# Transposing the query tile in two whole-tile instructions and a DRAM round trip, and a written-out order for all steps of the first MLP, in a linear-attention-then-two-MLPs kernel

## The chip, the cores and the metric

The kernel runs on one core of one Trainium2 chip. The metric is the device time of one execution in microseconds (us); smaller is better.

## The reference

Linear attention (8 batches, 8 heads, 576 positions, head size 64) is followed by two MLPs over the same 4608 tokens (512 to 2048 to 512 features).

```python
q_s = softmax(q, axis=-1)             # over the head's 64 features
k_s = softmax(k, axis=2)              # over the 576 positions
kv  = einsum('bhsd,bhse->bhde', k_s, v)
x   = einsum('bhsd,bhde->bhse', q_s, kv)      # -> (4608, 512)
x   = relu(x @ w_in1) ** 2 @ w_out1
h   = x @ w_in2
out = (h * sigmoid(1.702 * h)) @ w_out2
```

## The kernel before

**Precision and tiling.** Every large product is made in three passes of TensorE: an operand is cut into a rounded high part (`to_hi`, ScalarE) and the rest (`to_lo`, VectorE or GpSimd), and high*high, high*low and low*high are added up in PSUM. The first MLP goes over the tokens in 9 blocks of 512. In each block, 16 pieces `m{i}_{f}` (function `first`, tile `ph`, 12 matmuls of 512 columns) make hidden features, and 16 pieces `s{i}_{f}` (function `second`, tile `acc`, 12 matmuls) consume them `LAG = 2` pieces later. Between the two stand the steps `g.re`, `g.sq`, `g.hi`, `g.lo` (ReLU, square, and the two parts of the cut).

**What runs beside it.** While block i is multiplied, the attention of block i+1 is prepared, one pair of heads (p = 0 to 3) after another. The key steps `k{i}{p}.*` load k and v, find a maximum (`mx` on VectorE, `tr` on TensorE, `m2` on VectorE, `bc` on TensorE, `sb` on VectorE), take `ex` on ScalarE, multiply (`kv`, TensorE, tile `pk`), and normalise and cut the result (`su` on VectorE, `no` and `hi` on ScalarE, `lo` on GpSimd, tiles `kvn`, `kvh`, `kvl`). The query steps `x{i}{p}.*` load q, make its softmax (`mx`, `su` on VectorE, `sb`, `no` on GpSimd, `ex` on ScalarE), transpose it (`tr`), cut it (`hi` on ScalarE to `qh`, `lo` on VectorE to `ql`), multiply by the pair's `kvh` and `kvl` (`mm`, function `pe_x`, tile `px`) and put the result aside (`xe`). Near the end of a block `x{i}{p}.s` cuts the four results for the next block's `m` pieces. Besides this, the weights of the second MLP are widened from raw words (`w{n}.*`, tiles `ti`, `to`), stored, loaded again and turned into the seven combinations of a Strassen product (`f{n}.*`: sums `su` on VectorE, `hi` on ScalarE, `lo` on GpSimd, stores `d` by SyncE). The second MLP then uses these combinations.

**What sets the order.** Each engine works through its own queue in program order, and nearly all DMAs are issued by SyncE's queue (SP), which waits at a DMA until its data is there. The program of the opening (block 0, and the attention of block 1) follows a list written out by hand, `ORDER`. All steps after it are put into a list `plan` with planned times (for the attention the offsets `KV1` and `X1`, in units of `HS = 2.6` us, half of one m-and-s pair), moved by the amounts in `SHIFT`, and sorted by time.

**The transposition before.** For blocks 2 to 8 (7 blocks of 4 pairs: 28), `q_t` makes 16 VectorE transposes, each from one group of 32 partitions to another, so that features come to lie on partitions. The `qt` tile that they fill holds the tokens in another order than the products want, so `hi` and `lo` also put them in order: they write with a step of four elements (`by_token`). For blocks 0 and 1 TensorE transposes, and nothing of that changes.

Of the kernel before, what the change touches and what calls it, by code (L numbers as in the profile page):

```python
# [121 lines left out]
def kernel(  # L122
# [448 lines left out]
    def steps_x(i, p, ps, temp):  # L571

        st = {}
        G4 = P // 32
# [24 lines left out]
        def q_sum():
            r = st["m"][:, :, :, 1]  # L600
            nc.vector.reduce_sum(out=r, in_=st["q"], axis=AX.X)
            nc.vector.tensor_scalar_add(r, r, 1e-9)
            nc.vector.reciprocal(r, r)

        def q_norm():
            out = st["q"]
# [8 lines left out]
            st["qn"] = out

        def q_t():
            if i <= 1:  # L620
# [9 lines left out]
            st["qt"] = apool.tile([P, TB], F32, tag="qt", name=f"qt{i}_{p}", bufs=1)  # L630
            for a in range(G4):
                for g in range(G4):
                    h, e = divmod(g, 2)
                    nc.vector.transpose(  # L634
                        out=st["qt"][32 * g : 32 * g + 32, a * P : (a + 1) * P].rearrange(
                            "d (j t) -> d j t", j=QJ
                        ),
                        in_=st["qn"][32 * a : 32 * a + 32, h, :, 32 * e : 32 * e + 32],
                    )
            st["in"], st["out"] = "d (a j t) -> d a j t", "d (a t j) -> d a j t"  # L640

        def by_token(t):
            return t.rearrange(st["out"], j=QJ, **({"a": G4} if i > 1 else {}))

        def by_row(t):
            return t.rearrange(st["in"], j=QJ, **({"a": G4} if i > 1 else {}))
# [676 lines left out]
```

## Time and profile before

| | |
|---|---|
| median of 3 runs | 1617.09 us (1614.44, 1617.09, 1617.40) |
| the profiled execution's own time | 1616.54 us |
| its span, first to last instruction | 1614.8 us |
| TensorE matmuls busy | 1585.8 us (98% of the span) |
| VectorE (DVE) busy | 1104.6 us (68%) |
| GpSimd (POOL) busy | 902.9 us (56%) |
| ScalarE (ACT) busy | 764.1 us (47%) |

The span is what lies between the first and the last instruction; the execution's own time has 1.7 us more around it. Matmuls overlap in the pipeline and their ends are modelled, so 98% busy is no measure of how close TensorE is to its pace; the pace is read from the starts of equal pieces of work. In the rows PE is TensorE, PEld its weight loads, and L with a number is a line of the kernel.

### The profile page before, as it was taken

To read this page: it belongs to the slowest core of one execution; us is meant where nothing else is said; L and a number is where in the kernel's file an instruction comes from. 1 tells how busy PE (TensorE), PEld (TensorE's weight loads), DVE (VectorE), ACT (ScalarE), POOL (GpSimd) and SP (SyncE) were. 2 spreads that over 40 slices of the span, in tenths; PEclk is the share of its full clock that TensorE was granted. 3 is DMA by queue.
4 is the path that set the end of the run, shared out by engine and by line. 5 is a ranking of instruction groups with operands and counts; after the bars stand their busy time and mean duration, and the time that the engine had idled before them with its cause. 6 is when DMAs were issued, how large, how long until landed. Compare 5 with 4: busy or idle time off the path is not lost.

```text
span 1614.8 us, 23932 instructions
## 1 busy us (share of the span) xinstructions
PE 1585.8 (98%) x8132; PEld 1426.3 (88%) x8132; DVE 1104.6 (68%) x1952; ACT 764.1 (47%) x1481; POOL 902.9 (56%) x801
## 2 busy tenths in 40 slices
PE   7999999999999999999999999999999999999998
PEld 5888888878878888888888899999999999999997
DVE  7976777777776777767724356756756766676667
ACT  5874444344444444544443445445444544544432
POOL 6764355454554554555544556666566566566554
PEclk9999999999999999999999999999999999999999
DMA  9642345444443444423333387897897887987975
GB/s 270 212 125 84 108 131 158 128 143 138 133 143 118 153 133 133 141 92 124 118 131 137 124 297 264 257 326 256 252 332 252 262 319 253 285 302 242 298 254 152
DMA packets 216826, 314.07 MB, mean 195 GB/s; under 512 B 93312, under 2 KB 142464, under 8 KB 216704
## 3 DMA queue, kind: packets, MB, share of 16 engines
q1 hardware_dynamic: 210832, 308.34, 59.1%
q10 hardware_dynamic: 5872, 4.20, 0.9%
q8 instruction: 65, 1.06, 0.3%
q14 instruction: 57, 0.47, 0.1%
...
## 4 chain that ended last, share of the span: by engine, by line
PE 73%; DVE 12%; issue 6%; ACT 3%; POOL 3%; DMA 2%; SPq 0%; DVEq 0%; POOLq 0%; ACTq 0%
PE ps L724 15%; PE ph L724 14%; PE acc L724 14%; PE pcs L724 9%; PE pa L724 6%; PE pca L724 6%; DVE qt L634 4%; PE pls L724 3%; PE pla L724 3%; DVE g L751 1%; POOL x L202 1%; PE px L679 1%; PE pk L537 1%; POOL g L202 1%; DVE fi L375 1%
## 5 line engine op out<-in xcount | busy, mean ns | idle before, releaser
L724 PE MATMUL ph<-x,wi 128*128 128x512 f32 x1728 | 424.6, 393 | 2.2 <-POOL x L202 0.9
L724 PE MATMUL acc<-g,wo 128*128 128x512 f32 x1728 | 419.1, 391 | 0.5 <-DVE o L778 0.4
L724 PEld LDWEIGHTS ph<-x,wi 128*128 128x128 f32 x1728 | 320.2, 188 | 73.7 <-POOL x L202 3.1
L724 PEld LDWEIGHTS acc<-g,wo 128*128 128x128 f32 x1728 | 321.9, 188 | 67.7 <-DVE o L778 0.8
L202 POOL TENSOR_TENSOR g<-g,g 128x512 fp32r<-128x512 f32 x144 | 192.3, 1335 | 279.6 <-ACT g L199 194.8
L202 POOL TENSOR_TENSOR ga<-c,ga 128x384 fp32r<-128x384 f32 x144 | 154.5, 1082 | 153.5 <-ACT ga L199 95.3
L199 ACT ACTIVATE g<-g 128x512 fp32r<-128x512 f32 x144 | 91.0, 632 | 249.4 <-DVE g L751 249.3
L751 DVE TENSOR_TENSOR g<-g 128x512 f32<-128x512 f32 x128 | 105.3, 822 | 132.1 <-ACT g L745 128.2
L724 PE MATMUL pcs<-gs,ws 128*128 128x384 f32 x828 | 165.7, 334 | 0.0
L941 ACT ACTIVATE c<-c 128x384 f32<-128x384 f32 x144 | 75.7, 526 | 187.2 <-DVE c L932 187.2
L932 DVE TENSOR_TENSOR c<-ps,m 128x384 f32<-128x384 f32 x144 | 79.7, 553 | 117.8 <-PE ps L724 111.1
L202 POOL TENSOR_TENSOR gs<-c,gs 128x384 fp32r<-128x384 f32 x96 | 110.3, 1155 | 68.0 <-ACT gs L199 50.4
L724 PEld LDWEIGHTS pcs<-gs,ws 128*128 128x128 f32 x828 | 145.5, 188 | 0.0
L634 DVE STREAM_TRANSPOSE qt<-q 32x128 f32<-32x128 f32 x448 | 135.5, 302 | 8.8 <-POOL q L609 3.0
L202 POOL TENSOR_TENSOR gs<-s,gs 128x384 fp32r<-128x384 f32 x96 | 114.3, 1191 | 44.7 <-ACT gs L199 29.9
L745 ACT ACTIVATE g<-ph 128x512 f32<-128x512 f32 x144 | 86.0, 597 | 89.0 <-PE ph L724 85.6
L724 PE MATMUL pa<-a,w 128*128 128x384 f32 x576 | 115.7, 335 | 1.1 <-ACT m L925 0.4
L724 PE MATMUL ps<-s,wa 128*128 128x384 f32 x576 | 115.2, 334 | 0.0
L724 PE MATMUL pca<-ga,wa 128*128 128x384 f32 x552 | 110.6, 334 | 0.4 <-POOL ga L202 0.4
L724 PEld LDWEIGHTS pa<-a,w 128*128 128x128 f32 x576 | 101.0, 188 | 2.4 <-DVE c L932 0.9
L724 PEld LDWEIGHTS ps<-s,wa 128*128 128x128 f32 x576 | 101.2, 188 | 0.3 <-DVE c L932 0.2
L724 PEld LDWEIGHTS pca<-ga,wa 128*128 128x128 f32 x552 | 96.9, 188 | 0.7 <-POOL ga L202 0.7
(147 smaller groups left out, 2566.8 us busy)
## 6 DMA issues: line engine op xcount, KB each, us to landing
...
wb<-wiwb SPq DMA_DIRECT2D x48, 256.0 KB, 4.1
```

What stands on the lines that cost most here:

```text
L199: nc.scalar.activation(hi, src, AF.Copy)
L202: eng.tensor_tensor(out=lo, in0=src, in1=hi.bitcast(F32), op=ALU.subtract)
L375: nc.vector.tensor_tensor(out=block(*out), in0=block(*x), in1=block(*y), op=ALU.subtract)
L537: nc.tensor.matmul(st["pk"][:, :VW], st["ke"][:, j, :], st["v"][:, j, :], start=(j == 0), stop=(j == KJ),)
L634: nc.vector.transpose(out=st["qt"][32 * g : 32 * g + 32, a * P : (a + 1) * P].rearrange("d (j t) -> d j t", j=QJ), in_=st["qn"][32 * a : 3 ...
L679: nc.tensor.matmul(st["px"][:, cols], a, c[:, cols], start=(e == 0), stop=(e == 2))
L724: nc.tensor.matmul(out, w(a), x(b), start=(start and e == 0), stop=(stop and e == 2), skip_group_check=shared)
L745: nc.scalar.activation(st["g"], st["h"], AF.Relu)
L751: nc.vector.tensor_tensor(out=st["g"], in0=st["g"], in1=st["g"], op=ALU.mult)
L932: nc.vector.tensor_tensor(out=st[name], in0=st[at][:, :TH], in1=other, op=ALU.add)
L941: nc.scalar.activation(st[name], h, AF.Gelu_apprx_sigmoid)
```

## The change

Three things change. First, for blocks 2 to 8 `q_t` makes two VectorE transposes, each over all 128 partitions (its 32x32 squares stay in their group of 32 partitions), into a tile `tr`. A new step `wr` stores that tile to DRAM, and a new step `rd` loads it back with four DMAs, one for each group of 32 destination partitions, which brings the squares to their places. The loaded tile has the tokens in order, so `hi` and `lo` read and write without a step. Second, the buffers change: `tr` uses the buffer `qt`, the loaded tile uses the buffer `ql`, and the low part `ql` then takes the buffer `qt`. Third, a list `LATER` of 2097 steps, from the first steps of block 2's attention to the first products of the second MLP, sets the program order of these steps; all other steps follow in the order of their planned times as before.

```diff
+LATER = """
+k20.ld x20.ld k20.vl k21.ld k21.vl m1_0 k20.mx s0_14 x20.mx g1_0.re k21.mx x20.sb g1_0.sq k20.tr x20.ex m1_1 k20.m2
+g1_0.hi x20.su g1_0.lo x20.no s0_15 g1_1.re x20.tr g1_1.sq x20.wr p0 k20.bc m1_2 g1_1.hi g1_1.lo k20.sb x21.ld k20.ex
+x20.rd s1_0 g1_2.re g1_2.sq k22.ld g1_2.hi g1_2.lo k20.kv w0.ld x21.mx m1_3 x20.hi x21.sb k22.vl k20.su x20.lo k20.no
+k20.hi k22.mx x21.ex k20.lo x21.su s1_1 g1_3.re w0.ab g1_3.sq x21.no w0.b0 g1_3.hi g1_3.lo m1_4 w0.b1 w0.b2 k21.tr
+w1.ld s1_2 g1_4.re w0.st k21.m2 g1_4.sq g1_4.hi g1_4.lo x20.mm m1_5 x20.xe x21.tr w1.ab x21.wr w1.b0 x22.ld w1.b1
+w1.b2 k21.bc s1_3 g1_5.re k21.sb w1.st w2.ld g1_5.sq k21.ex x21.rd g1_5.hi x22.mx g1_5.lo m1_6 k23.ld x22.sb f0.ld
+x22.ex k21.kv w2.ab x22.su x21.hi s1_4 k23.vl g1_6.re w2.b0 x22.no k21.su x21.lo k21.no k21.hi f0.h.a11 k21.lo g1_6.sq
+f0.h.a12 f0.l.a11 f0.h.s4 m1_7 k23.mx g1_6.hi f0.l.a12 f0.d.a11 w2.b1 g1_6.lo f0.d.a12 w2.b2 s1_5 g1_7.re f0.l.s4
+g1_7.sq w3.ld w2.st f0.d.s4 f0.su g1_7.hi k22.tr x21.mm f0.h.s1 g1_7.lo f0.h.s3 f0.h.s2 m1_8 k22.m2 x21.xe x22.tr
...
-            st["qt"] = apool.tile([P, TB], F32, tag="qt", name=f"qt{i}_{p}", bufs=1)
-            for a in range(G4):
-                for g in range(G4):
-                    h, e = divmod(g, 2)
-                    nc.vector.transpose(
-                        out=st["qt"][32 * g : 32 * g + 32, a * P : (a + 1) * P].rearrange(
-                            "d (j t) -> d j t", j=QJ
-                        ),
-                        in_=st["qn"][32 * a : 32 * a + 32, h, :, 32 * e : 32 * e + 32],
-                    )
-            st["in"], st["out"] = "d (a j t) -> d a j t", "d (a t j) -> d a j t"
+            st["tr"] = apool.tile([P, G4, 32, QJ], F32, tag="qt", name=f"qt{i}_{p}", bufs=1)
+            for h in range(2):
+                nc.vector.transpose(
+                    out=st["tr"][:, 2 * h : 2 * h + 2].rearrange("d e t j -> d j e t"),
+                    in_=st["qn"][:, h].rearrange("p j (e d) -> p j e d", e=2),
+                )
+
+        def q_out():
+            nc.sync.dma_start(out=q_d[p], in_=st["tr"].rearrange("p g t j -> p (g t j)"))
+
+        def q_in():
+            st["qt"] = apool.tile([P, TB], F32, tag="ql", name=f"qd{i}_{p}", bufs=1)
+            turned = q_d[p].rearrange("(a d) (g c) -> g d a c", a=G4, g=G4)
+            for g in range(G4):
+                nc.sync.dma_start(
+                    out=st["qt"][32 * g : 32 * g + 32].rearrange("d (a c) -> d a c", a=G4), in_=turned[g]
+                )
+            st["in"], st["out"] = "d (n j) -> d n j", "d (n j) -> d n j"
...
-            st["ql"] = apool.tile([P, TB], F32R, tag="ql", name=f"ql{i}_{p}", bufs=1)
+            st["ql"] = apool.tile([P, TB], F32R, tag="qt" if i > 1 else "ql", name=f"ql{i}_{p}", bufs=1)
...
+    q_d = [dram.tile([P, TB], F32, name=f"qd{p}") for p in range(NP)]
...
-        plan.sort(key=lambda e: (e[0] + moved.get(shift_key(e[2]), 0.0), e[1]))
+        place = {e: n for n, e in enumerate(LATER.split())}
+        plan.sort(key=lambda e: (place.get(e[2], len(place)), e[0] + moved.get(shift_key(e[2]), 0.0), e[1]))
```

## Rows read from the trace of the kernel before

**Rows 1.** Stretches of blocks 1 to 7: start:end length, busy us (count) by engine.

```profile
core 0: us, PE busy (x) PEld busy (x) DVE busy (x) ACT busy (x) POOL busy (x), PEclk, DMA share, GB/s
126.37:223.69 97.32, 97.21 (x457) 80.59 (x456) 69.98 (x141) 41.03 (x77) 42.94 (x40) 1.00 0.34 100
223.69:322.52 98.83, 97.40 (x457) 80.15 (x456) 73.57 (x147) 43.64 (x85) 48.18 (x45) 1.00 0.49 147
322.52:423.10 100.58, 98.09 (x458) 79.78 (x456) 78.23 (x151) 45.83 (x90) 51.80 (x47) 1.00 0.44 134
423.10:522.32 99.22, 97.23 (x458) 80.22 (x456) 72.19 (x148) 43.73 (x86) 46.55 (x46) 1.00 0.44 138
522.32:621.59 99.27, 97.69 (x457) 80.42 (x456) 77.45 (x148) 47.58 (x88) 52.13 (x48) 1.00 0.44 138
621.59:719.47 97.88, 97.52 (x457) 80.78 (x456) 70.08 (x143) 46.55 (x85) 48.76 (x46) 1.00 0.41 129
719.47:809.84 90.37, 90.33 (x398) 74.20 (x396) 68.12 (x128) 40.87 (x71) 51.27 (x43) 1.00 0.32 110
```

**Rows 2.** Chain of waits in block 1: start, us, what.

```profile
129.25 2.72 PE acc L724 x12
131.98 0.11 PE pt L489
...
143.17 1.12 PE pk L537 x10
...
152.58 0.89 PE px L679 x6
```

**Rows 3.** What TensorE waited for, 120 to 905 us: us, times, longest.

```profile
PE px L679 <- ACT kvh L199: 2.2, 3, 1.7
PE pb L497 <- DVE mt L493: 1.0, 2, 0.6
```

**Rows 4.** Timeline in block 2: start us, us, engine line op, out<-in.

```profile
279.96 5.05 DVE L634 STREAM_TRANSPOSE qt<-q 32x128 f32<-32x128 f32 x16
...
284.50 1.28 PE L537 MATMUL pk<-vt,ke 128*128 128x130 f32 x10
285.03 0.81 SPq L579 DMA_DIRECT2D q<-in_q_dram  x2
...
293.27 0.15 DVE L547 TENSOR_SCALAR r<-pk 128x1 f32<-128x1 f32 x1
...
294.31 1.37 SPq L463 DMA_DIRECT2D vt<-in_v_dram  x2
...
294.58 0.39 PE L679 MATMUL px<-qh,kvh 128*128 128x256 f32 x1 [0.50 <-ACT kvn L554]
```

**Rows 5.** VectorE groups by shape: count, busy us, mean ns, idle before.

```profile
L634 DVE STREAM_TRANSPOSE qt<-q 32x128 f32<-32x128 f32 x448 | 135.5, 302 | 8.8 <-POOL q L609 3.0
...
L202 DVE TENSOR_TENSOR ql<-qt,qh 128x512 fp32r<-128x512 f32 x28 | 37.8, 1349 | 30.0 <-ACT qh L199 30.0
...
L1095 DVE STREAM_TRANSPOSE o<-suma 128x384 f32<-128x384 f32 x24 | 12.9, 554 | 0.1
```

**Rows 6.** ScalarE groups by shape.

```profile
L199 ACT ACTIVATE g<-g 128x512 fp32r<-128x512 f32 x144 | 91.0, 632 | 249.4 <-DVE g L751 249.3
...
L199 ACT ACTIVATE qh<-qt 128x512 fp32r<-128x512 f32 x28 | 31.1, 1112 | 0.0
```

**Rows 7.** DMA issues: count, KB each, median us from issue to landing.

```profile
y<-o SPq DMA_DIRECT2D x36, 256.0 KB, 2.9
...
vt<-in_v_dram SPq DMA_DIRECT2D x64, 128.0 KB, 3.5
...
fi<-wid SPq DMA_DIRECT2D x16, 256.0 KB, 3.4
...
q<-in_q_dram SPq DMA_DIRECT2D x8, 64.0 KB, 2.7
```

**Rows 8.** What SyncE's queue waited for, 120 to 905 us: us, times, longest.

```profile
SPq L404 <- POOL x L202: 339.0, 82, 11.6
```

More of the change, by code (lines that the diff above doesn't have):

```diff
@@ new lines @@
+k23.hi k23.lo g1_13.sq m1_14 g1_13.hi g1_13.lo s1_12 g1_14.re g1_14.sq g1_14.hi g1_14.lo x23.mm m1_15 x23.xe x30.tr
+x20.s x30.wr x31.ld f1.h.a11 x21.s x22.s s1_13 f1.h.s4 x23.s g1_15.re x30.rd f1.h.a12 g1_15.sq m2_0 f1.l.a12 x31.mx
+g1_15.hi f1.l.s4 f1.d.a12 g1_15.lo f1.d.s4 s1_14 x30.hi x31.sb g2_0.re x30.lo f1.l.a11 x31.ex g2_0.sq k30.tr m2_1
+f1.d.a11 k30.m2 g2_0.hi x31.su g2_0.lo f1.su x31.no s1_15 f1.h.s1 g2_1.re f1.h.s3 f1.h.s2 g2_1.sq f1.h.a22 p1 f1.l.s1
+k30.bc m2_2 g2_1.hi f1.l.s3 k30.sb g2_1.lo f1.d.s3 k30.ex k32.ld s2_0 f1.l.a22 g2_2.re f1.l.s2 f1.d.a22 g2_2.sq
@@ new lines @@
+f2.l.a22 f2.d.s3 k31.hi x32.su g2_6.hi m2_7 k31.lo f2.h.s2 f2.d.a22 w7.ab k33.mx g2_6.lo w7.b0 x32.no w7.b1 s2_5
+g2_7.re f2.l.s2 w7.b2 f2.l.s1 f2.d.s2 g2_7.sq w8.ld k32.tr w7.st x31.mm f2.d.s1 k32.m2 g2_7.hi m2_8 x32.tr x31.xe
+g2_7.lo x32.wr x33.ld s2_6 w8.ab f3.ld g2_8.re w8.b0 w8.b1 g2_8.sq x32.rd w8.b2 k32.bc g2_8.hi m2_9 k32.sb g2_8.lo
+f3.h.a11 x33.mx k32.ex k40.ld x33.sb f3.h.a12 w9.ld s2_7 f3.l.a11 x33.ex w8.st g2_9.re f3.l.a12 f3.d.a11 x33.su x32.hi
+f3.d.a12 g2_9.sq x33.no x32.lo k32.kv g2_9.hi g2_9.lo m2_10 k40.vl w9.ab k32.su k40.mx k32.no k32.hi w9.b0 k32.lo
@@ new lines @@
+w9.b1 s2_8 w9.b2 g2_10.re w9.st g2_10.sq g2_10.hi g2_10.lo m2_11 k33.tr s2_9 g2_11.re k33.m2 g2_11.sq g2_11.hi
+g2_11.lo x32.mm m2_12 x33.tr x32.xe x33.wr x40.ld k33.bc s2_10 g2_12.re k33.sb g2_12.sq k41.ld k33.ex g2_12.hi x40.mx
+x33.rd g2_12.lo m2_13 x40.sb k41.mx x40.ex k33.kv x40.su g2_13.re x33.hi s2_11 k41.vl k33.su x40.no x33.lo k33.no
+k33.hi k33.lo g2_13.sq m2_14 g2_13.hi g2_13.lo s2_12 g2_14.re g2_14.sq g2_14.hi g2_14.lo x33.mm m2_15 x33.xe x40.tr
+x30.s x40.wr x41.ld x31.s x32.s s2_13 f3.h.s4 x33.s g2_15.re x40.rd g2_15.sq m3_0 f3.l.s4 x41.mx g2_15.hi f3.su
@@ new lines @@
+f3.d.s4 x41.sb f3.h.s1 f3.h.s3 f3.h.s2 s2_14 x40.hi g3_0.re x40.lo g2_15.lo x41.ex g3_0.sq f3.h.a22 k40.tr m3_1
+f3.l.s1 k40.m2 g3_0.hi x41.su f3.l.s3 f3.d.s1 g3_0.lo f3.d.s3 s2_15 g3_1.re x41.no g3_1.sq f3.l.s2 p2 k40.bc m3_2
+f3.l.a22 g3_1.hi g3_1.lo k40.sb f4.ld k40.ex k42.ld s3_0 g3_2.re f3.d.s2 g3_2.sq f3.d.a22 w10.ld g3_2.hi f4.h.a11
+g3_2.lo k40.kv m3_3 f4.l.a11 k42.vl k40.su k42.mx k40.no k40.hi f4.h.a12 k40.lo f4.h.s4 f4.d.a11 f4.l.a12 s3_1 f4.l.s4
+f4.su f4.d.a12 g3_3.re w10.ab f4.d.s4 f4.h.s1 f4.l.s1 g3_3.sq f4.h.s3 m3_4 f4.l.s3 f4.d.s1 f4.h.s2 w10.b0 g3_3.hi
@@ new lines @@
+f4.l.s2 f4.d.s3 f4.h.a22 w10.b1 g3_3.lo f4.d.s2 k41.tr s3_2 w10.b2 g3_4.re f4.l.a22 k41.m2 w11.ld g3_4.sq w10.st
+x40.mm f4.d.a22 g3_4.hi m3_5 x41.tr x40.xe g3_4.lo x41.wr x42.ld k41.bc w11.ab s3_3 k41.sb g3_5.re g3_5.sq k43.ld
+k41.ex w11.b0 g3_5.hi w11.b1 x41.rd g3_5.lo m3_6 x42.mx w11.b2 x42.sb k43.mx w11.st w12.ld k41.kv x42.ex g3_6.re
+x42.su s3_4 x41.hi k43.vl k41.su x42.no x41.lo k41.no k41.hi f5.ld k41.lo g3_6.sq w12.ab m3_7 w12.b0 g3_6.hi w12.b1
+g3_6.lo w12.b2 f5.h.a11 f5.h.a12 s3_5 f5.l.a11 g3_7.re w13.ld f5.h.s4 g3_7.sq w12.st f5.l.a12 f5.d.a11 g3_7.hi f5.l.s4
@@ new lines @@
+f5.su f5.d.a12 k42.tr x41.mm g3_7.lo f5.d.s4 m3_8 x41.xe k42.m2 x42.tr w13.ab w13.b0 x42.wr w13.b1 s3_6 x43.ld g3_8.re
+w13.b2 g3_8.sq w14.ld w13.st g3_8.hi x42.rd k42.bc m3_9 g3_8.lo k42.sb x43.mx k42.ex k50.ld x43.sb s3_7 x43.ex g3_9.re
+x43.su w14.ab x42.hi g3_9.sq x43.no x42.lo k42.kv g3_9.hi g3_9.lo m3_10 k50.vl k42.su k50.mx k42.no k42.hi w14.b0
+k42.lo w14.b1 s3_8 w14.b2 g3_10.re w14.st g3_10.sq g3_10.hi g3_10.lo m3_11 k43.tr s3_9 g3_11.re k43.m2 g3_11.sq
+g3_11.hi g3_11.lo x42.mm m3_12 x43.tr x42.xe x43.wr x50.ld k43.bc s3_10 g3_12.re k43.sb g3_12.sq k51.ld k43.ex
@@ new lines @@
+g3_12.hi x50.mx x43.rd g3_12.lo m3_13 x50.sb k51.mx x50.ex k43.kv x50.su g3_13.re x43.hi s3_11 k51.vl k43.su x50.no
+x43.lo k43.no k43.hi k43.lo g3_13.sq m3_14 g3_13.hi g3_13.lo s3_12 g3_14.re g3_14.sq g3_14.hi g3_14.lo x43.mm m3_15
+x43.xe x50.tr x40.s x50.wr x51.ld f5.h.s3 x41.s x42.s s3_13 f5.h.s2 x43.s g3_15.re x50.rd f5.h.s1 g3_15.sq f5.h.a22
+m4_0 f5.l.s1 x51.mx g3_15.hi f5.l.s3 f5.d.s1 g3_15.lo f5.d.s3 s3_14 x50.hi x51.sb g4_0.re x50.lo f5.l.s2 x51.ex
+g4_0.sq k50.tr f5.l.a22 m4_1 f5.d.s2 k50.m2 g4_0.hi x51.su f6.ld g4_0.lo f5.d.a22 x51.no s3_15 g4_1.re g4_1.sq
@@ new lines @@
+f6.h.a11 p3 f6.l.a11 k50.bc m4_2 g4_1.hi f6.h.s4 g4_1.lo k50.sb f6.h.a12 f6.d.a11 k50.ex k52.ld f6.l.a12 s4_0 f6.l.s4
+f6.su g4_2.re f6.d.a12 f6.d.s4 f6.h.s1 f6.l.s1 w15.ld g4_2.sq k50.kv f6.h.s3 f6.d.s1 f6.l.s3 g4_2.hi k52.mx m4_3
+k52.vl g4_2.lo f6.h.s2 k50.su f6.h.a22 k50.no f6.l.s2 f6.d.s3 k50.hi f6.l.a22 f6.d.s2 s4_1 w15.ab k50.lo f6.d.a22
+g4_3.re w15.b0 w15.b1 g4_3.sq w15.b2 g4_3.hi m4_4 w15.st g4_3.lo w16.ld k51.tr s4_2 g4_4.re f7.ld k51.m2 g4_4.sq
+g4_4.hi w16.ab g4_4.lo x50.mm f7.h.a11 w16.b0 f7.h.a12 m4_5 f7.l.a11 f7.h.s4 x51.tr x50.xe f7.l.a12 w16.b1 f7.d.a11
@@ new lines @@
+x53.sb x53.ex s4_7 x52.hi x53.su g4_9.re g4_9.sq x53.no w19.ab x52.lo g4_9.hi k52.kv g4_9.lo k60.mx m4_10 k60.vl
+k52.su w19.b0 k52.no w19.b1 k52.hi w19.b2 k52.lo s4_8 w19.st g4_10.re g4_10.sq g4_10.hi g4_10.lo m4_11 k53.tr s4_9
+g4_11.re k53.m2 g4_11.sq g4_11.hi g4_11.lo x52.mm m4_12 x53.tr x52.xe x53.wr x60.ld k53.bc s4_10 g4_12.re k53.sb
+g4_12.sq k61.ld k53.ex g4_12.hi x60.mx x53.rd g4_12.lo m4_13 x60.sb k61.mx x60.ex k53.kv x60.su g4_13.re x53.hi s4_11
+k61.vl k53.su x60.no x53.lo k53.no k53.hi k53.lo g4_13.sq m4_14 g4_13.hi g4_13.lo s4_12 g4_14.re g4_14.sq g4_14.hi
@@ new lines @@
+g4_14.lo x53.mm m4_15 x53.xe x60.tr x50.s x60.wr x61.ld x51.s f7.h.s2 x52.s s4_13 x53.s g4_15.re f7.h.a22 x60.rd
+g4_15.sq m5_0 f7.l.s2 x61.mx g4_15.hi f7.l.a22 f7.d.s2 g4_15.lo f8.ld s4_14 f7.d.a22 x60.hi x61.sb g5_0.re x60.lo
+x61.ex g5_0.sq x61.su k60.tr g5_0.hi m5_1 f8.h.a11 g5_0.lo k60.m2 f8.h.a12 f8.h.s4 x61.no s4_15 f8.l.a12 g5_1.re
+f8.l.a11 f8.d.a12 g5_1.sq f8.l.s4 f8.d.a11 p4 k60.bc m5_2 g5_1.hi g5_1.lo k60.sb f8.d.s4 f8.su k60.ex k62.ld f8.h.s1
+s5_0 f8.h.s3 f8.l.s1 g5_2.re f8.h.s2 g5_2.sq f8.l.s3 f8.d.s1 w20.ld g5_2.hi k60.kv f8.h.a22 f8.l.s2 f8.d.s3 k62.mx
@@ new lines @@
+f12.l.a12 w26.b2 x73.ld s6_6 f12.d.a12 g6_8.re w27.ld w26.st g6_8.sq g6_8.hi x72.rd g6_8.lo k72.bc m6_9 x73.mx k72.sb
+x73.sb k72.ex x73.ex w27.ab s6_7 x73.su g6_9.re x72.hi g6_9.sq x73.no x72.lo g6_9.hi k72.kv g6_9.lo w27.b0 m6_10
+k72.su w27.b1 k72.no w27.b2 k72.hi k72.lo w27.st s6_8 g6_10.re g6_10.sq g6_10.hi g6_10.lo m6_11 k73.tr s6_9 g6_11.re
+k73.m2 g6_11.sq g6_11.hi g6_11.lo x72.mm m6_12 x72.xe x73.tr x73.wr x80.ld k73.bc s6_10 g6_12.re k73.sb g6_12.sq
+k73.ex x73.rd g6_12.hi x80.mx g6_12.lo m6_13 x80.sb x80.ex k73.kv x73.hi x80.su g6_13.re s6_11 x73.lo x80.no k73.su
@@ new lines @@
+g6_13.sq k73.no k73.hi k73.lo g6_13.hi m6_14 g6_13.lo s6_12 g6_14.re g6_14.sq g6_14.hi g6_14.lo x73.mm m6_15 x73.xe
+x80.tr x70.s x80.wr x81.ld x71.s x72.s s6_13 f12.h.s4 x73.s g6_15.re x80.rd g6_15.sq m7_0 f12.l.s4 x81.mx g6_15.hi
+f12.su x81.sb f12.d.s4 f12.h.s1 f12.h.s3 s6_14 x80.hi g7_0.re x80.lo g6_15.lo x81.ex g7_0.sq f12.h.s2 f12.h.a22 m7_1
+f12.l.s2 x81.su g7_0.hi f12.l.a22 f12.d.s2 g7_0.lo f12.d.a22 s6_15 g7_1.re x81.no g7_1.sq f12.l.s1 p6 m7_2 g7_1.hi
+f12.l.s3 g7_1.lo f13.ld f12.d.s3 s7_0 f12.d.s1 g7_2.re g7_2.sq g7_2.hi w28.ld g7_2.lo m7_3 f13.h.a12 f13.h.s4
@@ new lines @@
+f14.l.a11 w30.b1 s7_5 f14.l.a12 f14.d.a11 g7_7.re w30.b2 f14.l.s4 f14.d.a12 g7_7.sq w31.ld w30.st x81.mm f14.d.s4
+f14.su g7_7.hi m7_8 x81.xe g7_7.lo x82.tr x82.wr w31.ab x83.ld s7_6 g7_8.re w31.b0 w31.b1 g7_8.sq w31.b2 g7_8.hi
+x82.rd m7_9 g7_8.lo x83.mx x83.sb w31.st s7_7 x83.ex g7_9.re x83.su act g7_9.sq x83.no g7_9.hi m7_10 x82.hi g7_9.lo
+x82.lo s7_8 g7_10.re g7_10.sq g7_10.hi g7_10.lo m7_11 s7_9 g7_11.re g7_11.sq g7_11.hi g7_11.lo x82.mm m7_12 x83.tr
+x82.xe x83.wr s7_10 g7_12.re g7_12.sq x83.rd g7_12.hi g7_12.lo m7_13 s7_11 x83.hi g7_13.re x83.lo g7_13.sq g7_13.hi
@@ new lines @@
+m7_14 g7_13.lo s7_12 g7_14.re g7_14.sq g7_14.hi g7_14.lo x83.mm m7_15 x83.xe late b0.ld x80.s f14.h.s3 x81.s s7_13
+x82.s x83.s g7_15.re f14.h.s2 g7_15.sq f14.h.a22 m8_0 f14.h.s1 f14.l.s3 b0.h.a11 g7_15.hi f14.l.s2 f14.d.s3 g7_15.lo
+f14.d.s2 s7_14 g8_0.re f14.l.a22 g8_0.sq f14.l.s1 f14.d.a22 g8_0.hi m8_1 b0.s1 f15.ld f14.d.s1 g8_0.lo s7_15 g8_1.re
+b0.l.a11 f15.h.a11 g8_1.sq f15.h.a12 p7 f15.l.a11 m8_2 f15.h.s4 g8_1.hi f15.l.a12 g8_1.lo f15.d.a11 f15.d.a12 s8_0
+f15.l.s4 f15.su g8_2.re b0.s3 f15.d.s4 f15.h.s1 g8_2.sq m8_3 v0.w1 f15.h.s3 f15.h.s2 f15.l.s1 f15.h.a22 b0.s2 s8_1
@@ L97, in shift_key @@
+g8_11.hi g8_11.lo m8_12 s8_10 g8_12.re g8_12.sq g8_12.hi g8_12.lo m8_13 s8_11 g8_13.re g8_13.sq g8_13.hi g8_13.lo
+m8_14 s8_12 g8_14.re g8_14.sq g8_14.hi g8_14.lo m8_15 b0.h.s4 b0.l.s4 s8_13 g8_15.re g8_15.sq g8_15.hi g8_15.lo n0.a11
+n0.s2 n0.m1 s8_14 n0.+c12 n0.a12 n0.s3 v1.w1 n0.a.c11 n0.h.a11 s8_15 n0.+c22 n0.l.a11 p8 n0.s1 n0.a22 n0.++c22 v1.wa
+n0.a.c22 n0.s4 n0.+c21 n0.h.a22 n0.a.c21 n1.a11 n0.l.a22 n0.++c12 n0.a.c12
+"""
 def shift_key(label):
@@ L173 @@
     KV1 = [HS * t for t in (-4, -3.9, -0.9, 1.1, 2.0, 3.0, 3.7, 3.75, 5.7, 6.6, 6.6, 6.6, 6.6)]
-    X1 = [HS * t for t in (-2, 0.1, 0.1, 1.1, 2.1, 2.1, 4.1, 6.1, 6.1, 8.3, 9.0)]
+    X1 = [HS * t for t in (-2, 0.1, 0.1, 1.1, 2.0, 2.0, 3.0, 3.4, 4.7, 6.4, 6.4, 8.5, 9.0)]
     PT = 1.04
@@ L629, in q_t @@
                 return
[L630 to L640 removed]
+            st["tr"] = apool.tile([P, G4, 32, QJ], F32, tag="qt", name=f"qt{i}_{p}", bufs=1)
[14 more added lines that the diff above has]
+            st["in"], st["out"] = "d (n j) -> d n j", "d (n j) -> d n j"
         def by_token(t):
[L643 removed]
+            return t.rearrange(st["out"], j=QJ)
         def by_row(t):
[L646 removed]
+            return t.rearrange(st["in"], j=QJ)
         def q_whole():
@@ L695, in steps_x @@
         whole = dict(hi=q_whole, mm=pe_whole) if i == 0 else dict(hi=q_hi, lo=q_lo, mm=pe_x)
+        move = dict(wr=q_out, rd=q_in) if i > 1 else {}
         return dict(
-            ld=load, la=on_act(load), mx=q_max, sb=q_sub, ex=q_exp, su=q_sum, no=q_norm, tr=q_t, **whole, **last,
+            ld=load, la=on_act(load), mx=q_max, sb=q_sub, ex=q_exp, su=q_sum, no=q_norm, tr=q_t, **move, **whole, **last,
         )
```

51 lines of the change are left out of this document (added).

## The prediction

> **What bounds the kernel now.** I read the stretches first, one for each block of the first MLP [rows 1]. TensorE's weight loads count 456 in each of blocks 1 to 6, so the work is the same, yet the blocks take 97.32, 98.83, 100.58, 99.22, 99.27 and 97.88 us. The clock is fully granted in all of them, so the difference is waiting. What a block would take without a wait comes from the chain of waits in a stretch where TensorE feeds itself [rows 2]: a piece of 12 matmuls starts 2.72 us before the next, a step `tr` or `bc` takes 0.11, a `kv` 1.12 and a query product `mm` 0.89. A block has 32 pieces, eight `tr` or `bc`, four `kv` and four `mm`: 32 x 2.72 + 8 x 0.11 + 4 x 1.12 + 4 x 0.89 = 95.96 us. The six blocks lose 1.36, 2.87, 4.62, 3.26, 3.31 and 1.92 us to waits, 17.3 in all. Block 7, with no keys to prepare, should take 32 x 2.72 + 4 x 0.89 = 90.6 and takes 90.37: it loses nothing.
>
> The reader should see two more things. The loss follows VectorE's busy time: 70 us busy go with 1.4 and 1.9 us lost, 78.2 with 4.6 [rows 1]. And what TensorE waits for (nine rows, 7.4 us in all, from 2.2 for `kvh` down to 0.4) are steps at the end of chains that pass through VectorE: `kvh`, `mt`, `ke`, `x`; two of the nine stand in [rows 3]. The rest of the 17.3 us does not show as idle time, since the ends of matmuls overlap the next start. Block 2 shows one such place [rows 4]: the product `pk` is done at 285.78, but VectorE, after 5.05 us of transposes and what they have pushed back, comes to its reciprocal step only at 293.27, and the query product at 294.58 has waited for what hangs on it.
>
> **The change part by part.** *Transposes.* Removed are 16 of 302 ns at a pitch that makes 5.05 us per pair [rows 4, 5], 28 times. Added are two over 128 partitions x 256 elements. The nearest rows are of the same operation: 128 elements take 302 ns and 384 take 554 [rows 5], which is 0.98 ns per element and 428 ns for 256. That is the lower bound. The new transposes write with a step of four elements; ScalarE's cut with such a step takes 1112 ns where the plain one takes 632 [rows 6], 0.94 ns more per element, which gives 668 ns as the upper bound. I take 0.55 us each, 1.1 per pair.
>
> [...]
>
> *The cuts.* `lo` on VectorE took 1349 ns [rows 5], `hi` on ScalarE 1112 [rows 6]. Both become plain: `hi` 632, and `lo`, scaled alike, 1349 x 632 / 1112 = 767 ns (bounds: nothing gained, and this). Per pair VectorE gives up 5.05 + 1.35 and takes 1.1 + 0.77: 4.5 us saved, 18 per block, 127 over 28 pairs. ScalarE saves 0.48 per pair, 13 in all. None of this lies on TensorE; it counts only through the waits.
>
> *The round trip.* A pair adds five DMAs on SP. SP spends 0.81 us on two small query loads and 1.37 on two value loads [rows 4], so 0.4 to 0.7 each and 2 to 3.5 us per pair, hidden unless something behind them is late. The store is like `y<-o`, 2.9 us to landing; the loads are like the 64 KB query load, 2.7, or at most like `fi<-wid`, 3.4 [rows 7]. The fourth load is issued 3 x 0.45 = 1.35 after the first. From the start of the transposes to a ready `ql` this is 1.1 + 2.9 + 1.35 + 2.7 + 0.63 + 0.77 = 9.5 us (8.9 to 11.5 with the bounds).
>
> What room has it? `tr` writes the buffer that the pair before reads in `mm`, so it cannot begin sooner. In the list the narrowest gap between two `mm` (pairs 0 to 1 and 2 to 3) has six pieces, a `bc`, a `kv` and a `tr`: 6 x 2.72 + 2 x 0.11 + 1.12 = 17.7 us [rows 2]. That leaves 8.2 us for waits in queues. In the widest, from pair 3 to the next block's pair 0, there are twelve pieces. So the round trip is hidden if SP is punctual.
>
> *The order.* I went through the list against the starts of TensorE's pieces. TensorE's own order stays but for one thing: `mm` of pairs 0 and 2 comes one piece later, which gives `kvh` and `kvl` 2.72 us more where TensorE waits for them. The loads `k.ld`, `x.ld` and their first steps come up to a dozen pieces earlier; the four `g` steps come about one piece later, but are used two m-and-s pairs later; the `f` steps and their stores come some seven pieces earlier. Each of these moves frees its successor, and the price is what now stands before it in its queue. On ScalarE `hi` now waits for a load, and behind it stand `no` and `hi` of the keys, and `re` of the next piece. On VectorE `tr` waits for the `mm` before, and behind it stands `sb`. On SP, `rd` waits until `wr` has landed, and behind it stand the raw weights and the next loads, none of which is due at once.
>
> **The sum.** The forecast rests on the trend of rows 1: between 78.2 and 70.0 us of VectorE time a block loses 0.4 us less per us saved. With 18 us saved, blocks 2 to 6 come to about 52 to 60 us, below any of them, and the trend leaves nothing of the 17.3 us. This is the upper bound; the lower is nothing. I take three quarters, 13.0 us, because every pair gets a new wait for DMA that rows 1 don't contain. Opening and second MLP keep their order and are put at nothing. The profiled execution goes from 1616.54 to 1603.5, its span from 1614.8 to 1601.8; the median, 0.55 above it now, from 1617.09 to about 1604.
>
> **The rivals.** *The round trip comes late (slower).* SP's stores of the combinations wait for GpSimd 82 times, 4.1 us on average and up to 11.6 [rows 8], and whatever is queued behind waits too. If `wr` and `rd` each meet an average wait, 8.2 us, the room of 8.2 is just used up. If one meets the longest, the pair is 3.4 late; in half of the 28 pairs the gap is a narrow one, and there 0.93 us of lateness at each eats the 13 gained: beyond that the kernel is slower. At 1.7 us each it loses 24 and gives 1628. Against it: in the list only few stores stand between `wr` and `rd`. Chance 0.12.
>
> *The four loads go one after another.* If loads to different partition groups did not overlap, they would take 4 x 2.7 = 10.8 us in place of 4.05, the chain 16.2, and 1.5 us would be left for SP's waits; with an average wait of 4.1 each narrow pair is 2.6 late, 36 us, and the time 1640. The rows speak against it: the value loads of 128 KB, issued in twos on different columns, land after 3.5 us in the median, about as long as one load of 256 KB, 3.4 [rows 7]. [...] Chance 0.04.
>
> *The waits move.* VectorE gets free, but `kvh`, `kvl` and the block's first `x` hang on ScalarE and GpSimd too [rows 3], and ScalarE now stops at `hi`. Then only a third is won, 6 us: 1611. For it: the key chain's places on TensorE don't change. Chance 0.14.
>
> *VectorE's time was slack.* The trend of rows 1 is then only a common effect of a bad order, and the new one has as many bad places: 1617. Against it: block 7 has 68 us of VectorE's work in 90 and loses nothing, so load alone isn't the cause; for it, the same. Chance 0.09.
>
> **How the numbers follow.** The forecast keeps 0.61, with its own range 1599 to 1609 (all 17.3 us, to 8 of them). The median is told from no change at about 0.2%, 3.2 us. Faster: 0.61 + 0.14 = 0.75; the same: 0.09; slower: 0.12 + 0.04 = 0.16. The range reaches from 1599 to 1617: beyond lie the slower cases, 0.16, and a few hundredths below for gains outside the six blocks.
>
> **What would show it.** Blocks 2 to 6 of 96 to 97.5 us with VectorE busy 52 to 60; transposes of 0.43 to 0.67 us, 56 of them; `hi` at 632 and `lo` near 770 ns; the round trip within 7 to 9 us; ScalarE's waits for the loaded tile short of TensorE. Wrong would be: TensorE waiting at `px` for `qh` or `ql`, SP's waits between `wr` and `rd` above 8 us, or blocks as long as before while VectorE is idle.

## The result, and the profile after

The changed kernel takes 1601.81 us (median of 4 runs, 1598.73 to 1602.24) where the kernel before takes 1617.24 beside it: a ratio of 0.9903, 95% interval 0.9885 to 0.9921. The forecast was 1604. The profiled execution went from 1616.54 to 1601.90 us, its span from 1614.8 to 1600.1.

The stretches of blocks 1 to 7 in the kernel after (columns as in [rows 1], which these answer to):

```profile
127.14:223.69 96.55, 96.55 (x457) 80.60 (x456) 62.32 (x96) 43.02 (x83) 46.57 (x43) 1.00 0.49 146
223.69:319.82 96.13, 96.13 (x458) 80.28 (x456) 60.15 (x92) 43.94 (x85) 50.02 (x47) 1.00 0.54 164
319.82:415.68 95.86, 95.86 (x458) 79.96 (x456) 63.34 (x96) 45.43 (x89) 50.91 (x46) 1.00 0.53 162
415.68:511.81 96.13, 96.13 (x458) 80.28 (x457) 57.48 (x92) 43.58 (x85) 49.56 (x47) 1.00 0.53 165
511.81:608.35 96.54, 96.54 (x458) 80.61 (x457) 58.20 (x89) 47.78 (x87) 49.86 (x46) 1.00 0.51 161
608.35:705.54 97.19, 97.02 (x457) 80.69 (x456) 57.88 (x87) 45.47 (x84) 51.87 (x48) 1.00 0.43 142
705.54:795.49 89.95, 89.95 (x397) 74.36 (x396) 46.48 (x67) 42.02 (x73) 44.92 (x39) 1.00 0.43 141
```

Blocks 1 to 6 take 578.4 us together where they took 593.1; without a wait they would take 575.8 (six times the pace of 95.96). So 14.7 of the 17.3 us are won, block 7 gives 0.4 more, and the stretches ahead of block 1 and behind block 8 are as long as before within 1 us. What TensorE waited for between 120 and 905 us is down to three rows, 1.3 us in all where it was 7.4 (us, times, longest; answers to [rows 3]):

```profile
PE pa L871 <- ACT m L1072: 0.6, 1, 0.6
PE pca L871 <- POOL ga L340: 0.5, 1, 0.5
PE pk L675 <- ACT ke L670: 0.2, 1, 0.2
```

The new instructions, from VectorE's and ScalarE's groups by shape (count, busy us, mean ns, idle before; answers to [rows 5, 6]):

```profile
L770 DVE STREAM_TRANSPOSE qt<-q 128x256 f32<-128x256 f32 x56 | 30.8, 627 | 39.1 <-PE px L824 35.8 <-POOL g L340 2.1 <-POOL q L747 1.2
...
L340 DVE TENSOR_TENSOR ql<-qd,qh 128x512 fp32r<-128x512 f32 x28 | 29.1, 1039 | 16.0 <-ACT qh L337 15.4
```

```profile
L337 ACT ACTIVATE qh<-qd 128x512 fp32r<-128x512 f32 x28 | 17.5, 626 | 12.8 <-DMA qd<-qd 12.7
```

And one round trip, from the timeline in block 1 (start us, us, engine line op):

```profile
177.92 1.10 DVE L770 STREAM_TRANSPOSE qt<-q 128x256 f32<-128x256 f32 x2
...
179.05 0.32 SPq L776 DMA_DIRECT2D qd<-qt  x1
...
182.68 2.02 SPq L782 DMA_DIRECT2D qd<-qd  x4
...
187.22 0.63 ACT L337 ACTIVATE qh<-qd 128x512 fp32r<-128x512 f32 x1 [3.86 <-DMA qd<-qd]
...
187.89 0.69 DVE L340 TENSOR_TENSOR ql<-qd,qh 128x512 fp32r<-128x512 f32 x1 [4.63 <-ACT qh L337]
```

The reader is to see that ScalarE stood 3.86 us before the cut and VectorE 4.63 before the next one, and that TensorE has no row of waits for `qh` or `ql`. The transposes come in pairs of 1.10 us, as forecast. Store and loads land after 2.1 and 2.0 us in the median:

```profile
qd<-qt SPq DMA_DIRECT2D x28, 256.0 KB, 2.1
qd<-qd SPq DMA_DIRECT2D x112, 64.0 KB, 2.0
```

### The profile page after: what moved, and what is told of

It reads as the page before. It is cut to its first block, busy times and chain, and to the rows that moved or that the text cites. A ratio compares the mean times of both kernels' runs of the same rounds, so it can differ in the third digit from the quotient of the medians.

```text
span 1600.1 us, 23876 instructions
## 1 busy us (share of the span) xinstructions
PE 1576.3 (99%) x8132; PEld 1424.9 (89%) x8132; DVE 1003.4 (63%) x1560; ACT 762.1 (48%) x1481; POOL 906.6 (57%) x801
## 4 chain that ended last, share of the span: by engine, by line
PE 89%; DVE 4%; DMA 3%; ACT 1%; SPq 1%; issue 1%; POOL 1%; DVEq 0%; POOLq 0%; ACTq 0%
PE ph L871 22%; PE acc L871 22%; PE ps L871 14%; PE pcs L871 8%; PE pa L871 6%; PE pca L871 5%; PE pls L871 3%; PE pla L871 3%; PE pk L675 2%; PE px L824 2%; SPq L1251 1%; DMA q<-in_q_dram 1%; DMA w<-wiw 1%; DVE o L1242 1%; DMA fo<-wod 0%
## 5 line engine op out<-in xcount | busy, mean ns | idle before, releaser
L898 DVE TENSOR_TENSOR g<-g 128x512 f32<-128x512 f32 x128 | 110.6, 864 | 124.9 <-ACT g L892 119.8
L1221 DVE TENSOR_TENSOR sums<-pcs,sums 128x384 f32<-128x384 f32 x102 | 56.7, 556 | 49.6 <-PE pcs L871 49.0
```

The source lines that it names most:

```text
L898: nc.vector.tensor_tensor(out=st["g"], in0=st["g"], in1=st["g"], op=ALU.mult)
L1221: nc.vector.tensor_tensor(out=o, in0=bank, in1=o, op=ALU.add)
```

## The experiments

Two theories stood at first. V: the VectorE time that the new transposition frees took TensorE's waits away. O: the new order did. Several runs came out as neither foresaw; the text says which. Each time below is a median of 4 runs (10 in the runs e9 and e11), with its ratio to the kernel before measured on the same chip. Before was 1617.8 to 1618.9 us there.

### The order alone, and the transposition alone

The first run (e1) keeps the list and goes back to the old transposition and buffers.

```diff
-            st["tr"] = ...; two transposes; wr; rd
+            st["qt"] = ...; 16 transposes of 32 partitions, as before; no wr, no rd
```

> The new order with the old transposition (16 VectorE transposes per pair, no round trip, the cuts with a step). Theory V, VectorE's freed time took the waits away: VectorE is busy 68 to 80 us in each of blocks 1 to 6 again, the six blocks lose some 12 to 17 us again, the time is 1612 to 1618. Theory O, the order took them away: the blocks stay within 1 us of 96 and the time is 1600 to 1604. Half and half would be about 1609.

Measured: 1630.78 us, ratio 1.0079 (1.0064 to 1.0094). Slower than before, and outside what either theory expected. Two of its stretches (blocks 1 and 5):

```profile
126.36:230.94 104.58, 99.21 (x457) 81.36 (x456) 82.48 (x165) 43.97 (x83) 47.44 (x43) 0.98 0.39 111
...
524.90:627.90 103.00, 99.35 (x457) 82.64 (x456) 73.68 (x145) 48.77 (x87) 51.10 (x46) 0.97 0.42 131
```

TensorE waits 17.0 us at nine key products, and a piece of the timeline shows why:

```profile
PE pk L675 <- ACT ke L670: 17.0, 9, 3.6
```

```profile
182.93 0.28 DVE L631 TENSOR_REDUCE mt<-pt 128x1 f32<-128x128 f32 x1
183.13 5.03 DVE L772 STREAM_TRANSPOSE qt<-q 32x128 f32<-32x128 f32 x16
...
190.47 0.82 DVE L646 TENSOR_TENSOR ke<-kt,pb 128x640 f32<-128x640 f32 x1
...
191.31 0.74 ACT L670 ACTIVATE ke<-ke 128x640 f32<-128x640 f32 x1 [0.70 <-DVE ke L646]
...
192.10 1.41 PE L675 MATMUL pk<-vt,ke 128*128 128x130 f32 x10 [3.04 <-ACT ke L670]
```

On VectorE the list puts `tr` between `m2` and `sb` of the keys (`mt` and `ke` in these lines) in 19 of 24 places. With 5.03 us of transposes there `sb` starts at 190.47, and the key product waits; with the changed kernel's 1.1 us it waits 0.2 us in one place in all.

The second run (e2) has the new transposition and round trip and the planned times. The change also moved offsets in `X1` (`tr` 2.9 us earlier, the two cuts 0.8 and `mm` 0.5 later), and e2 keeps these new values. So it is not the kernel before with another transposition alone.

```diff
-        plan.sort(key=lambda e: (place.get(e[2], len(place)), e[0] + moved.get(...), e[1]))
+        plan.sort(key=lambda e: (e[0] + moved.get(...), e[1]))
```

> The new transposition and round trip with the planned times instead of the list. Theory V: the blocks lose less than 5 us in all, the time is 1601 to 1607. Theory O: the old waits stay, and the round trip brings new ones at the query product; the six blocks lose 12 us or more, the time is 1613 or above.

Measured: 1642.23 us, ratio 1.0149 (1.0134 to 1.0164). VectorE is busy only 51 to 60 us in each of blocks 1 to 6, and they lose 36 us. Blocks 3 and 6, the most and the least of VectorE's time:

```profile
329.04:432.38 103.34, 98.31 (x457) 80.74 (x456) 59.53 (x96) 44.21 (x89) 49.73 (x47) 0.98 0.50 151
...
636.38:738.12 101.74, 97.14 (x458) 80.60 (x456) 51.43 (x87) 43.74 (x82) 46.45 (x44) 1.00 0.45 142
```

The longest wait of TensorE there, ScalarE's wait for the loaded tile, SyncE's before the stores of the combinations, and one place in block 2:

```profile
PE pb L635 <- DVE mt L631: 22.1, 7, 5.3
```

```profile
ACT qh L337 <- DMA qd<-qd: 94.3, 26, 9.0
```

```profile
SPq L542 <- POOL x L340: 274.6, 66, 12.0
```

```profile
249.84 0.63 ACT L337 ACTIVATE qh<-qd 128x512 fp32r<-128x512 f32 x1 [9.03 <-DMA qd<-qd]
```

ScalarE stands before a tile that has not landed, VectorE stands 6.6 us behind ScalarE, and `m2` of the keys is queued behind that. Theory O had the time right (1613 or above) but looked for the new waits at the query product; TensorE waits there for `qh` once, 3.1 us. And TensorE works through its pieces in the same sequence as in the changed kernel: the 40 us between the two lie in the queues of the other engines.

So neither theory holds alone: each part by itself makes the kernel slower, by 13 and by 24 us, and the two together make it 15 faster. The change of buffers went along with the transposition and was not tried by itself.

### The move of the query product

In the run e3 the changed kernel has `mm` of pairs 0 and 2 one piece earlier, where it was.

```diff
-... k21.tr w1.ld s1_2 g1_4.re ... x20.mm m1_5 ...
+... k21.tr w1.ld x20.mm s1_2 g1_4.re ... m1_5 ...
```

> The changed kernel with the query product of pairs 0 and 2 one piece of 12 matmuls earlier, as it stood before; all else as changed. If that move of 2.72 us was what freed the product of its wait for the cut keys, TensorE waits at it again, up to 10 us over 14 products (1605 to 1612). If the keys are ready in any case, within 1 us of the changed kernel (1601 to 1603).

Measured: 1600.95 us, ratio 0.9895 (0.9880 to 0.9909). The move is worth nothing inside the changed kernel; the keys' parts are ready in any case.

### VectorE's time inside the new order

The run e4 fills the same tile with 16 transposes; order, buffers and round trip stay.

```diff
-            for h in range(2):
-                nc.vector.transpose(out=st["tr"][:, 2 * h : 2 * h + 2]..., in_=st["qn"][:, h]...)
+            for a in range(G4):
+                for g in range(G4):
+                    nc.vector.transpose(out=st["tr"][32 * a : 32 * a + 32, g]..., in_=st["qn"][32 * a : 32 * a + 32, h, :, 32 * e : 32 * e + 32])
```

> The changed kernel, but with 16 transposes of 32 partitions into the same tile, so that order, buffers and round trip stay and VectorE has some 4 us per pair more to do, on the way to the store. Theory V: VectorE is busy 73 to 80 us per block, the blocks lose 8 to 17 us, the time is 1610 to 1618. Theory O: 1601 to 1605, with at most the round trip some 4 us later than in the changed kernel.

Measured: 1632.12 us, ratio 1.0096 (1.0074 to 1.0119), 30 us above the changed kernel and above what either theory expected. TensorE waits at the same place as with the order alone:

```profile
PE pk L675 <- ACT ke L670: 15.8, 9, 2.8
```

This is the time of the order alone, 1630.78, to 1.3 us, though that run has no round trip, the old buffers and cuts with a step. So within the new order, with long transposes, these three together are worth next to nothing; the short transposes are worth the 30 us. The 16 are not the same as before, either. They now write with a step of four elements and stay in their group of partitions:

```profile
L772 DVE STREAM_TRANSPOSE qt<-q 32x128 f32<-32x128 f32 x448 | 122.3, 380 | 21.1 <-PE px L826 18.8 <-POOL q L747 1.2
```

Each takes 380 ns where it took 302 [rows 5], yet 16 of them are done in 4.4 us where they took 5.05 [rows 4].

Is it the load, or that it comes in one piece? The run e9 spreads the load: a second VectorE instruction behind each square.

```diff
-                nc.vector.tensor_tensor(out=st["g"], in0=st["g"], in1=st["g"], op=ALU.mult)
+                for op in (ALU.mult, ALU.max):
+                    nc.vector.tensor_tensor(out=st["g"], in0=st["g"], in1=st["g"], op=op)
```

> The changed kernel with a second VectorE instruction behind each square of the first MLP's blocks 1 to 8 (the maximum of the tile with itself, which changes nothing), 0.69 us or more each, 11 to 14 us of VectorE time per block, in 16 small pieces. VectorE is then as busy as in the kernel before, some 70 to 77 us per block. If its load makes the waits, whatever its form, the time is 1620 or above, as with the 16 transposes. If only the long uncut stretch of transposes did, within 4 us of the changed kernel (1600 to 1606).

Measured: 1620.34 us, ratio 1.0018 (1.0009 to 1.0028), 18.5 above the changed kernel and just what was expected if the load counts in any form (1620 or above). The stretches of blocks 3 and 6:

```profile
324.83:421.21 96.38, 96.00 (x457) 79.82 (x456) 77.43 (x112) 44.28 (x89) 50.24 (x45) 1.00 0.54 161
...
618.97:719.73 100.76, 98.03 (x457) 80.73 (x456) 69.04 (x103) 45.93 (x84) 50.31 (x48) 1.00 0.42 137
```

The first, the busiest of blocks 1 to 6 with 77.43 us of VectorE time, loses 0.4 us to waits; the second, with 69.04, loses 4.8. So more VectorE time costs, in one piece or spread, but a block's total doesn't say how much: what counts is what comes late in which place. (The second instruction also lengthens the chain of `g` steps; TensorE's longest wait is again for `ke`, 6.0 us in six places.)

The run e7 tries to take the 5 us out of the bad place. It is the order alone, but in the 19 places where `tr` stands between `m2` and `sb` it comes after `sb`; the next pair's first steps move along, on all engines.

```diff
-... k22.m2 x21.xe x22.tr ... x23.ld ... k22.sb x23.mx ...
+... k22.m2 x21.xe ... k22.sb x22.tr ... x23.ld ... x23.mx ...
```

> The new order with the old 16 transposes, as in the run with the order alone, but in the 19 places where they stand on VectorE between the key steps m2 and sb they come after sb (the next pair's first steps move along). Theory P, what counts is what stands behind the 5 us: TensorE's 17 us of waiting for ke at the key product go away, and the time falls from 1631 to 1605 to 1615, at the same VectorE load. Theory L, the load itself: it stays at 1625 to 1635.

Measured: 1641.99 us, ratio 1.0149 (1.0130 to 1.0168). The wait for `ke` is down from 17.0 us to 1.2 in one place, as expected, but the time went up by 11 us and lies above both theories. Other waits have taken its place, the longest at the hidden features:

```profile
PE ph L847 <- DVE x L323: 8.7, 5, 2.7
```

So the one bad place explains where the order alone stalls, but moving the 5 us, with the steps that move along, only moves the stall.

### The room of the round trip

Three runs copy the stored tile from DRAM to DRAM one, two or four times before it is loaded (e11, e5, e6).

```diff
+            for hop in range(N):
+                nc.sync.dma_start(out=q_hop[hop][p], in_=(q_hop[hop - 1] if hop else q_d)[p])
-            turned = q_d[p].rearrange(...)
+            turned = q_hop[-1][p].rearrange(...)
```

> The changed kernel with two more hops in the round trip (the stored tile is copied twice from DRAM to DRAM before it is loaded), some 5 to 7 us later per pair by the 2.1 us landing of the store and the issue. If the room of 8.2 us that the prediction worked out is right, this is about hidden: within 3 us of the changed kernel (1600 to 1605). If the round trip is on the edge already, each narrow pair loses 3 us or more: 1640 and above.

> The changed kernel with four more hops, 10 to 14 us later per pair. With a room of 8.2 us the narrow pairs (14) come 2 to 6 us late at TensorE: 1630 to 1690. If the room is larger than worked out, less than 1615; if steps queued behind the cut on ScalarE and VectorE matter more than the query product itself, TensorE waits at the key products and at the hidden features, not at the query product.

> The changed kernel with one more hop in the round trip, about 3.5 us later per pair by the landing and issue of the hops measured with two. If ScalarE's waiting at the cut is paid in full from the first microsecond, about half of what two hops cost: 1630. If there is a small room of 2 to 4 us, 1602 to 1612.

Measured: one hop 1616.95 us, ratio 0.9993 (0.9982 to 1.0004); two hops 1665.02, 1.0301 (1.0280 to 1.0321); four hops 1836.24, 1.1342 (1.1309 to 1.1375). A hop lands after 3.2 us where there is one, and after 3.0 and 2.9 where there are two. One costs 15 us and eats the whole gain, more than the 2 to 4 us of room would have allowed and less than half of two; two cost 63, four 234, more than any branch had, and with four TensorE waits at the query product too (13.1 us for `qh`, 37.9 for `kvh`). ScalarE's wait at the cut, 12.7 us in the changed kernel, becomes 158.3 with two hops, and with one:

```profile
ACT qh L337 <- DMA qd<-qh0d: 79.2, 27, 5.9
```

With one hop TensorE doesn't wait at the query product for `qh` or `ql` at all. Its longest wait there is again the key product:

```profile
PE pk L675 <- ACT ke L670: 5.4, 5, 3.4
```

A hop delays two things: the cut, and whatever is queued behind the loads on SyncE, which now stands until the hop has landed:

```profile
SPq L784 <- DMA qh0d<-qd: 83.4, 28, 5.0
```

Block 1 shows the second. With one hop, and then the same steps in the changed kernel:

```profile
144.17 1.73 SPq L784 DMA_DIRECT2D qd<-qh0d  x4
...
147.13 0.60 SPq L400 DMA_DIRECT2D rawi<-in_moe_w_in_dram  x1
...
161.43 0.66 ACT L408 ACTIVATE ti<-rawi 128x512 f32<-128x512 f32 x1 [3.57 <-DMA rawi<-in_moe_w_in_dram]
...
163.92 0.81 DVE L646 TENSOR_TENSOR ke<-kt,pb 128x640 f32<-128x640 f32 x1
...
165.56 1.39 PE L675 MATMUL pk<-vt,ke 128*128 128x130 f32 x10 [1.05 <-ACT ke L670]
```

```profile
144.37 0.59 SPq L400 DMA_DIRECT2D rawi<-in_moe_w_in_dram  x1
...
160.69 0.81 DVE L646 TENSOR_TENSOR ke<-kt,pb 128x640 f32<-128x640 f32 x1
...
165.21 1.28 PE L675 MATMUL pk<-vt,ke 128*128 128x130 f32 x10
```

The load of raw weight words is issued 2.8 us later. ScalarE's and VectorE's widening steps wait for such loads in turn, `sb` of the keys is queued behind them, and it starts 3.2 us later. Followed back in this way through the profile, 6.8 us of TensorE's 7.5 us in longer waits (over 0.2 us) with one hop lead to loads that SyncE issued late, and 0.7 to the cut. With two hops 20.2 of 37.7 lead to the cut and 13.1 to SyncE's queue, and with four most lead to the cut. This is a reading of three profiles; no run delays the cut and leaves SyncE free.

So the room is not what the query product leaves. At one hop it is used up by what stands behind the round trip in SyncE's queue, and the changed kernel has little of it left; how much the steps behind the cut would leave by themselves stays open.

### Why planned times don't carry the round trip

Three runs start from the transposition alone. The run e8 plans the two cuts 3.1 us later, e10 plans load to round trip 2.6 us earlier and the cuts 1.3 later, and e12 plans the stores of the combinations 3.0 later.

```diff
-    X1 = [HS * t for t in (-2, 0.1, 0.1, 1.1, 2.0, 2.0, 3.0, 3.4, 4.7, 6.4, 6.4, 8.5, 9.0)]
+    X1 = [HS * t for t in (-2, 0.1, 0.1, 1.1, 2.0, 2.0, 3.0, 3.4, 4.7, 7.6, 7.6, 8.5, 9.0)]      # e8
+    X1 = [HS * t for t in (-3, -0.9, -0.9, 0.1, 1.0, 1.0, 2.0, 2.4, 3.7, 6.9, 6.9, 8.5, 9.0)]    # e10
+    ... e[0] + moved.get(...) + (3.0 if re.match(r"f\d+\.d", e[2]) else 0.0) ...                 # e12
```

> The new transposition with planned times, as in the run with the transposes alone, but both cuts hi and lo planned 3.1 us later. If the loss there came from ScalarE and VectorE standing in front of a load that had not landed (94 us of waits at hi in 26 places), most of it goes: 1605 to 1625. If the planned order is bad in itself beside the round trip, it stays at 1635 or above.

> The new transposition with planned times, as in the run with the transposes alone, but load to round trip planned 2.6 us earlier and the two cuts 1.3 us later. If planned times can serve the round trip when they give it room, most of the loss goes: 1605 to 1620. If ScalarE and VectorE still meet the loaded tile too early or TensorE the cuts too late, 1630 or above.

> The new transposition with planned times, as in the run with the transposes alone (1642 us), but the stores of the Strassen combinations planned 3.0 us later, so that SyncE's queue stands less before stores whose data is not there (275 us in 66 places). If that standing is what makes the round trip late under planned times, SyncE's wait falls to under 120 us, ScalarE's wait for the loaded tile (94 us) to under 50, and the time to 1610 to 1628. If the round trip is late for another cause, ScalarE's wait stays near 90 us and the time at 1635 or above.

Measured: e8 1638.01 us, ratio 1.0127 (1.0110 to 1.0144); e10 1642.68, 1.0156 (1.0141 to 1.0171); e12 1634.33, 1.0106 (1.0083 to 1.0129). With the cuts later, VectorE stands 21.8 us behind ScalarE at the cut where it stood 103.4 in e2, and TensorE's wait for `mt` falls from 22.1 to 1.8 us, but the cuts come too late for the query product, which waits 7.0 us for `qh` and longer for `ql`:

```profile
PE px L824 <- DVE ql L340: 10.2, 14, 1.2
```

With the start earlier, VectorE stands 65.7 us before query loads that have not landed. With the stores later, SyncE's standing before them halves and the kernel is some 8 us faster than e2. That is between the two outcomes expected for it:

```profile
SPq L542 <- POOL x L340: 136.3, 41, 11.6
```

```profile
ACT qh L337 <- DMA qd<-qd: 66.1, 19, 8.9
```

In the changed kernel ScalarE waits 12.7 us at the cut, and SyncE's two longest waits are these:

```profile
SPq L776 <- DVE qt L770: 152.3, 23, 15.3
SPq L542 <- POOL x L340: 85.5, 59, 5.8
```

Standing before the stores of the combinations is thus a part of what makes the round trip late under planned times, a third of the 24 us by the time. But it is not that SyncE stands less in the changed kernel: between 120 and 905 us it stands 483 us there, 487 in e2 and 484 in e12. It stands elsewhere. The list puts the round trip's own store early in SyncE's queue, so that SyncE waits for the transposes (152.3 us) and issues the store at once when they end. From their end to the last load in place it takes 7.4 us on average over the 28 pairs, 9.0 in e2 and 7.9 in e12. These 1.6 us are less than what ScalarE's wait at the cut differs by, 2.9 us per pair; the rest must lie in where the list puts the cut. These are readings of the profiles, and no run separated them. What e8 and e10 show is that the two offsets tried, one for all pairs, don't find a place for the cuts.

## Why the prediction was right or wrong

**The loss and its place: right.** The working found 17.3 us of waits in blocks 1 to 6 and none elsewhere worth counting. 14.7 of them are gone, the pace of 95.96 us is reached to 0.1 to 1.2 us, and nothing outside these blocks changed by more than 1 us. Three quarters were taken; it was 85%, so the time came out 2 us below the forecast. That it came out so near is in part luck: the sum rests on the trend below, which is no cause.

**The transposes and cuts: mostly right.** The two transposes took 627 ns each, inside 428 to 668 and above the 550 taken, but their pitch gave the 1.10 us per pair. In the run e4 the small transposes with a step took 380 ns where those without took 302; these also stay in their group of partitions, so the step is not alone in it. The measured 627 is nearer to the upper bound of 668 than to 428. `hi` took 626, as forecast. `lo` took 1039 on average, not 767, though the one at 187.89 took 0.69 us; so it gave back 0.3 us per pair, not 0.6. VectorE's busy time fell by 7.7 to 19.3 us per block, 13.7 on average, not by 18, and blocks 2 to 6 lie at 57 to 63 us, not at 52 to 60.

**The trend between VectorE's time and the loss: failed as a reason.** It gave the right sum, but it is no law. Under the transposition alone VectorE is busy 51 to 60 us and blocks 1 to 6 lose 36 us; under the spread load, 77.4 us go with 0.4 us lost and 69.0 with 4.8. What the runs put in its place: inside the new order VectorE's time does matter (30 us for the 16 transposes, 18.5 for the spread load), and it is paid at the key chain `m2`, `sb`, `ex`, `kv`. TensorE's longest wait is for `ke` in every run that slows something inside the new order at its places (17.0 us in the run e1, 15.8 in e4, 6.0 in e9, 5.4 in e11), and 0.2 us in the changed kernel.

**The room of the round trip, 8.2 us: wrong.** The duration was nearly right: from the store's issue to the cut it is 8.2 us in the place shown (179.05 to 187.22) and 8.1 in the median of the 28 pairs, with 18 of them inside 7 to 9 and the rest from 5.5 to 11.1. From the start of the transposes to a ready `ql` the median is 11.1 us where 9.5 were worked out, because, on average, the loads are issued 0.8 us after the store has landed and the cut starts 0.7 us after the last load, two waits that the sum left out, and the cuts take 0.6 us longer. (By the terms as given, the bounds of that sum are 9.1 to 11.7.) But the room was measured to the query product alone. Of what stands behind `rd` in SyncE's queue the prediction said that none is due at once, and put it at nothing; it also named the steps behind `hi` and `tr` and priced none. One hop with a landing of 3.2 us costs 15 us, and its profile leads most of the waits back to the raw weights and other loads that SyncE issued late. The rival of the late round trip therefore had its deciding point much nearer than worked out; with the transposition under planned times it is what happens. In the changed kernel it didn't happen, as its profile shows: the store is issued at once when the transposes end, and the cut is placed where ScalarE waits 12.7 us for it in all.

**The order: right in direction, wrong in detail.** The move of `mm` by 2.72 us, the one change in TensorE's order, is worth nothing in the changed kernel. And the prediction took order and transposition as two helps that add up. Neither helps alone: the order needs short transposes, and the round trip needs the order.

**The four loads.** The rival in which they run one after another is ruled out. In the place shown they were issued 0.5 us apart, from 182.68 on; each landed 2.9 to 3.4 us after its issue, which end to end would be 12.6 us, but all were in place 4.5 us after the first issue. In all 28 pairs every load was issued before the one ahead of it had landed. These readings are of issue and landing only, so whether the loads' bytes took turns on the way can't be told from them.
